# The last rows of wo in a decode kernel: the last row in two halves, row 0 added ahead of the merge

## The chip, the cores and the metric

One core of one Trainium2 chip runs the whole kernel. The metric is device microseconds of one execution, the median over several runs. The profiler also gives one execution in detail: which instruction ran when on which engine, what it waited for, and what the DMA engines moved.

## The reference

One decode step mixes two branches for two batch rows: attention over a cache of 4096 keys and values for 32 heads, and a small feed-forward branch with SiLU.

```
g = _sigmoid((x * gate_w).sum(-1, keepdims=True))
q = (x @ wq).reshape(B, Sq, H, Dh)          # B=2, Sq=1, D=640, H=32, Dh=128
p = softmax(einsum("bhqd,bhkd->bhqk", q, k_cache) * Dh ** -0.5)
a = einsum("bhqk,bhkd->bhqd", p, v_cache).reshape(B, Sq, H * Dh) @ wo    # wo: 4096 x 640
b = silu(x @ w1) @ w2
out = g * a + (1 - g) * b                    # 2 x 1 x 640
```

All data is float32. Keys and values are 268 MB together, wo is 10.5 MB.

## The kernel before

The heads go in groups of four (HQ = 8), with two batch rows: 16 items. For each item a key slab and a value slab of 128 partitions by 16384 numbers are loaded; GpSimd and VectorE multiply keys by the query, VectorE sums to scores, ScalarE exponentiates, TensorE multiplies weights by values. The results, scaled by the gate, stand in the tile oP, 32 columns for each row of wo that a partition holds.

After the last item comes the projection by wo. Every partition holds 32 rows of wo in four groups (NP = 4) of PR = 8 rows, each of 640 numbers. Groups 0 to 2 go to the slab v, the last group (g = 3) to the slab b. `load_wo` issues six DMAs from SyncE's queue: groups 0 and 1 together, group 2 in two pieces, group 3 in three (rows 0 to 4, rows 5 and 6, row 7). A float32 matmul shows in the trace as two matmul records, two passes one after the other.

- `in_halves` (L556) takes a row in two halves of 320 columns, in two strips of 32 PSUM partitions, and adds it up in the bank ps_acc (`early`), where the feed-forward branch already stands. Groups 0 and 1 use two pairs of strips at once; group 2 uses one pair.
- `merge` (L568, L573): ScalarE copies `early` to SBUF (`partial`), and four matmuls with the constant `join` sum the halves up into the bank ps_0 (`acc`), now in four strips of 160 columns.
- `in_quarters` (L586) takes each row of the last group in four strips of 160 columns, straight into `acc`.
- VectorE copies `acc` to SBUF (`ot`, L891), and SyncE's last DMA stores it to the output in pieces of 640 bytes.

The order on each engine is the order of the code. `Flow.op` finds the waits: an operation waits for the last writer of what it reads and for the readers of what it writes. Of PSUM banks it has a rule more, which the prediction needs:

```
if r.startswith("ps_"):
    deps += [d for d in self.readers.get(r, ()) if d.eng != eng]
```

So an engine that reads a PSUM bank waits for readers of the same bank on other engines that stand ahead of it in the code. A wait of TensorE for a piece of wo stands ahead of the first matmul that reads the piece, and holds up whatever TensorE has behind it.

Of the kernel before, what the change touches and what calls it, by code (L numbers as in the profile page):

```python
# [5 lines left out]
ALU = mybir.AluOpType  # L6
AX = mybir.AxisListType
# [151 lines left out]
def gated_decode(nc, x, kc, vc, wq, wo, w1, w2, gate, out):  # L159
    P = 128  # L160
    B, H, SK, DH = kc.shape
    D = x.shape[2]
# [13 lines left out]
    HB = 16  # L176
    CV = 68
    G = 4
    W = D // G
    W2 = D // 2  # L180
    NP = HQ // 2
    PR = 2 * Q
    FIRST = 5
    LEAD = HB // 2
    PACED = (NP - 2) * PR
    items = [(hq, b) for hq in range(HQ) for b in range(B)]
# [3 lines left out]
    s_out, s_sent = nc.alloc_semaphore("output"), nc.alloc_semaphore("sent")  # L190
    f = Flow(nc)
    V, S_, T_, G_ = nc.vector, nc.scalar, nc.tensor, nc.gpsimd

    def sb(name, shape, align=32):
        return nc.alloc_sbuf_tensor(name, shape, F32, align_bytes=align)[tuple([slice(None)] * len(shape))]

    def bank(name):
        return nc.alloc_psum_tensor(name, [P, 512], F32)[:, :]
# [4 lines left out]
    slab = {n: slabs[:, k * SLAB : (k + 1) * SLAB] for k, n in enumerate("vba")}  # L203

    def part(n, *ks):
        return [f"{n}.{k}" for k in (ks or range(8))]
# [13 lines left out]
    g = sb("g", [P, B])  # L220
# [4 lines left out]
    he = sb("he", [P, FR, B])  # L225
    seq = sb("seq", [P, 2 * FR, HB])
    join = sb("join", [P, 2, HB + 1])
    turned = sb("turned", [P, FR * 32])
    mask = sb("mask", [P, B])
    spaced = sb("spaced", [P, FR, 32])  # L230
# [7 lines left out]
    row = sb("row", [64, DH])  # L238
    oP_xs = sb("oP_xs", [P, LEAD + NP * PR * 32 + D // Q])
    oP, xs = oP_xs[:, : -D // Q], oP_xs[:, -D // Q :]  # L240
# [3 lines left out]

    ps_q, ps_o, ps_v, ps_acc, ps_t, ps_m, ps_0, ps_1 = (bank(f"ps{i}") for i in range(8))
    oT = ps_m[:64, 256:512].rearrange("p (n r) -> p n r", r=32)
    early, acc = ps_acc[:, :W2], ps_0[:, :W]

    h_q, h_e, h_v, h_o = (f.sem(n) for n in ("next_q", "weights", "values", "rows"))

# [4 lines left out]
    PD = PR * D  # L255


    partial = slab["v"][:, (NP - 1) * PD :][:, :W2]
    ot = slab["v"][:, (NP - 1) * PD + W2 :][:, :W]

    def kslab(i):
        return "a" if i % 2 == 0 else "b"
# [21 lines left out]
    def load_wo(g):  # L284

        n, at = ("v", g * PD) if g < NP - 1 else ("b", 0)
        if g == 0:
            src = wo[: 2 * PR * P, :].rearrange("(g p n) d -> p g (n d)", g=2, n=PR)
            to = slab["v"][:, : 2 * PD].rearrange("p (g c) -> p g c", g=2)
            f.dma("SP", to, src, writes=part("v", 0, 1), after=v_users)  # L290
            return
        if g == 1:
            return
        src = wo[g * PR * P : (g + 1) * PR * P, :].rearrange("(p n) d -> p (n d)", n=PR)
        cuts = (0, PD // 2, PD) if g < NP - 1 else (0, FIRST * D, PD - D, PD)
        after = f.users(part(n)) if g == NP - 1 else v_users
        for k, (c0, c1) in enumerate(zip(cuts, cuts[1:])):
            f.dma("SP", slab[n][:, at + c0 : at + c1], src[:, c0:c1], writes=part(n, g % (NP - 1) + k), after=after)
# [11 lines left out]
        writes=part("v", 0),  # L310
# [7 lines left out]
            out=ident, in_=ident, compare_op=ALU.not_equal, fill=1.0, base=0, pattern=[[-1, P]], channel_multiplier=1  # L318
        ),
        reads=["ident"],  # L320
        writes=["ident"],
# [2 lines left out]
    f.op("POOL", lambda: G_.memset(pz, 0.0), writes=["pz"])  # L324
    f.op("POOL", lambda: G_.memset(seq, 0.0), writes=["seq"])

    out_rows = out.rearrange("b s (n d) -> (s n) b d", n=G)
    f.dma("SP", out_rows, oP[0:P:HB, :W], reads=["oP"], writes=["out"])

    f.op("DVE", lambda: V.memset(ones, 1.0), writes=["ones"])  # L330
    f.op(
# [2 lines left out]
        reads=["ident"],  # L334
        writes=["block"],
# [6 lines left out]
        reads=["block"],  # L342
        writes=["fold"],
# [4 lines left out]
        reads=["ident"],  # L348
        writes=["sel"],
# [4 lines left out]
        reads=["ident"],  # L354
        writes=["half"],
# [7 lines left out]
            axis=AX.X,  # L363
        ),
        reads=["sel"],
        writes=["pick"],
# [4 lines left out]
        reads=["sel"],  # L371
        writes=["own"],
# [4 lines left out]
        reads=["ident"],  # L377
        writes=["side"],
# [6 lines left out]
        reads=["block"],  # L385
        writes=["spread"],
# [4 lines left out]
        reads=["ident"],  # L391
        writes=["mask"],
    )
    f.op("DVE", lambda: V.memset(join, 0.0), writes=["join"])
    for e in range(2):
        ends, at = join[:, e, ::HB], 64 + HB * (1 - e)
# [5 lines left out]
            reads=["ident", "join"],  # L402
            writes=["join"],
        )
        for t in (at, at + 32):
# [3 lines left out]
                reads=["ident", "join"],  # L409
                writes=["join"],  # L410
            )

    H_AT = FH * HD
    X_AT = H_AT + B * F
# [4 lines left out]
        reads=["xs0", "xs1"],  # L421
        writes=["xt"],
# [5 lines left out]
        reads=["xt"],  # L428
        writes=["gx"],
# [7 lines left out]
    for b in range(B):  # L437
        for j in range(J):
            at = xt[:, j, HB * b : HB * b + 1]
# [11 lines left out]
                reads=part("a") + ["xt"],  # L451
                writes=[f"hsum{b}"],
            )

    def mm_hr():
# [18 lines left out]
        reads=["ones", "gp"],  # L474
        writes=["ps_o"],
# [7 lines left out]
        reads=["g"],  # L483
        writes=["gc"],
# [7 lines left out]
    for e in range(2):  # L492
# [3 lines left out]
            reads=["ps_v"],  # L496
            writes=[f"spaced{e}"],
# [8 lines left out]
        reads=["he", "gc"],  # L506
        writes=["he"],
    )
    for e in range(2):
# [5 lines left out]
            reads=["he", "turned", "half", "seq"],  # L515
            writes=[f"seq{e}"],
# [27 lines left out]
    def heads(g):  # L544
        return [f"oP{g}{u}{b}" for u in range(2) for b in range(B)]

    def in_halves(g):

        for k in range(PR):
            s_ = g * PR + k  # L550

            def fn(k=k, s_=s_):
                to = 64 * (s_ % 2) if s_ < PACED else 0
                for n in range(2):
                    at = 32 * s_ + LEAD // 2 * n
                    last = T_.matmul(  # L556
                        early[to + 32 * n : to + 32 * n + 32, :],
                        oP[:, at : at + 32],
                        slab["v"][:, s_ * D + n * W2 : s_ * D + (n + 1) * W2],
                        start=(s_ == 0),  # L560
                        stop=(s_ in (PACED - 1, PACED + PR - 1)),
                    )
                return last

            f.op("PE", fn, reads=part("v", g + (g == NP - 2 and k >= PR // 2)) + heads(g), writes=["ps_acc"])

    def merge():
        f.op("ACT", lambda: S_.copy(partial, early), reads=["ps_acc"], writes=["partial"])  # L568

        def fn():  # L570
            for n in range(G):
                e, c = divmod(n * W, W2)
                last = T_.matmul(  # L573
                    acc[32 * n : 32 * n + HB + 1, :], join[:, e, :], partial[:, c : c + W], start=True, stop=False
                )
            return last

        f.op("PE", fn, reads=["partial", "join"], writes=["ps_0"])

    def in_quarters(g):  # L580
        for k in range(PR):
            at = LEAD + 32 * (g * PR + k)

            def fn(k=k, at=at):
                for n in range(G):
                    last = T_.matmul(  # L586
                        acc[32 * n : 32 * n + HB + 1, :],
                        oP[:, at : at + HB + 1],
                        slab["b"][:, k * D + n * W : k * D + (n + 1) * W],
                        start=False,  # L590
                        stop=(k == PR - 1),
                    )
                return last

            f.op("PE", fn, reads=part("b", (k >= FIRST) + (k == PR - 1)) + heads(g), writes=["ps_0"])

    ffn_out("v")

# [40 lines left out]
    def copy_q(i):  # L639
        f.op("ACT", lambda: S_.copy(qsb, ps_q[:, :DH]), reads=["ps_q"], writes=["qsb"])  # L640

    f.op("PE", mm_qr, reads=part("v", 1) + part("b") + ["xz"], writes=["ps_0", "ps_1"])
    for u in range(2):
        for b in range(B):
# [7 lines left out]
                reads=[f"ps_{u}", "mask"],  # L652
                writes=[f"qall{u}{b}"],
# [199 lines left out]
    for i in range(N + 1):  # L853
# [22 lines left out]
        if i == N - 1:  # L876
            v_users = f.users(part("v"))
            for g_ in range(NP):
                load_wo(g_)
# [4 lines left out]
        if i + 1 < N:  # L884
            query(i + 1, by=[ops["relay", i]], loop=i)
            copy_q(i + 1)
    for g_ in range(NP - 1):
        in_halves(g_)
    merge()
    in_quarters(NP - 1)  # L890
    f.op("DVE", lambda: V.tensor_copy(ot, acc), reads=["ps_0"], writes=["ot"])  # L891
    f.dma("SP", out_rows, ot[0:P:HB, :], reads=["ot"], writes=["out"], signal=s_out)


    def land():
# [15 lines left out]
    f.plan()  # L911
    for e in ("SP", "POOL"):
        f.run(e)
    spans = {"ACT": (14, 34), "DVE": (100, 220), "PE": (len(f.ops["PE"]) - NP * PR - 1, len(f.ops["PE"]))}
    for e, (a, b) in spans.items():
        ops, at = f.ops[e], 0
        while at < len(ops):
            end = at
            if at == a:
                f.once(e, ops[a:b])  # L920
                at = b
            elif ops[at].loop is None:
# [3 lines left out]
                at = end  # L926
            else:
# [3 lines left out]
                at = end  # L931
# [21 lines left out]
```

## Time and profile before

| | before |
|---|---|
| median of 3 runs | 695.7 us (695.59 to 695.74) |
| span of the profiled execution | 694.2 us |
| what lies around the span, against the median | 1.5 us |
| TensorE, VectorE, ScalarE, GpSimd busy | 30%, 73%, 6%, 38% of the span |
| moved from memory | 298.26 MB, 430 GB/s over the span |

The profiled execution has no time of its own on record beside its span, so a span is set against the median with the 1.5 us as a constant. Times within the execution are us from the start of the span. Busy shares are means over a long loop and a short end; what this change touches is the last six us.

### The profile page before, as it was taken

What the parts mean: (1) busy time and instruction counts of PE and PEld (TensorE: products, weight loads), DVE (VectorE), ACT (ScalarE), POOL (GpSimd) and SP (SyncE); (2) the same over time, 40 slices, a digit from 0 to 9 for tenths busy, and PEclk for the clock granted to TensorE, in tenths of its full rate; (3) what the DMA queues carried; (4) which work ended last, traced back from release to release, by engine and by line L of the source; (5) the groups of instructions that cost most, each with busy time, mean ns of one, the idle gap of its engine ahead of it and who ended that gap; (6) DMA issues with size and microseconds to landing.
All of it is one profiled execution on the core that took longest, in us unless ns stands there. A gap on an engine that the chain in (4) does not pass through costs nothing. (4 is left out here: it accounts for less than half of the span.)

```text
span 694.2 us, 3593 instructions
## 1 busy us (share of the span) xinstructions
PE 211.4 (30%) x1440; PEld 72.5 (10%) x1440; DVE 507.5 (73%) x269; ACT 40.0 (6%) x152; POOL 265.6 (38%) x26
## 2 busy tenths in 40 slices
PE   0074032151331405060412306060503315050657
PEld 0032010010110101020100101010100101010113
DVE  3810958898989596886959596986959595977811
ACT  0001010101010101010010101010000101010000
POOL 1000808191726090815335180906244270907100
PEclk9998556565565757575665757575655757575689
DMA  9999999999999999999999999999999999999997
GB/s 383 430 446 450 430 427 424 423 457 438 427 430 423 430 461 427 434 423 423 438 457 427 430 423 427 464 430 430 423 423 461 434 430 427 423 438 457 427 408 326
DMA packets 6209, 298.33 MB, mean 430 GB/s; under 512 B 672, under 2 KB 700, under 8 KB 956
## 3 DMA queue, kind: packets, MB, share of 16 engines
q1 hardware_dynamic: 6204, 298.27, 99.4%
q8 instruction: 2, 0.03, 0.0%
q14 instruction: 3, 0.02, 0.0%
HBM read 298.26 MB, written 0.01 MB: 430 GB/s over the span
## 5 line engine op out<-in xcount | busy, mean ns | idle before, releaser
L670 POOL TENSOR_TENSOR slabs<-slabs,qsb 128x7680 f32<-128x7680 f32 x16 | 262.3, 16396 | 378.7 <-DMA slabs<-in_A_k_cache_dram 347.8
L686 DVE TENSOR_REDUCE s<-slabs 128x68 f32<-128x8704 f32 (+1 forms) x32 | 276.3, 8676 | 0.0
L766 PE MATMUL ps<-slabs,pz 128*32 128x512 f32 x1024 | 146.2, 735 | 345.2 <-PEq L145 338.2
L676 DVE TENSOR_TENSOR slabs<-slabs,ps 128x8704 f32<-128x8704 f32 x16 | 147.5, 9218 | 108.5 <-DMA slabs<-in_A_k_cache_dram 108.4
L766 PEld LDWEIGHTS ps<-slabs,pz 128*32 128x32 f32 x1024 | 39.5, 132 | 438.6 <-issue 431.6
L715 ACT ACTIVATE pz<-s,nb 32x128 f32<-32x128 f32 x64 | 25.4, 398 | 556.5 <-PE ps L766 363.2
L804 PE MATMUL ps<-osb,pick 128*128 128x512 f32 x32 | 20.4, 724 | 58.9 <-PEq L145 58.0
L818 DVE TENSOR_REDUCE row<-ps 64x128 f32<-64x512 f32 x16 | 10.9, 682 | 23.3 <-PE ps L804 23.3
L788 DVE SCALAR_TENSOR_TENSOR osb<-ps,rg,own 128x512 f32<-128x512 f32 x16 | 12.0, 748 | 21.4 <-PE ps L766 21.2
L618 PE MATMUL ps<-qall,spread 128*128 (+1 forms) x32 | 7.4, 319 | 35.3 <-PEq L145 34.5
L446 DVE SCALAR_TENSOR_TENSOR slabs<-slabs 128x1728 f32<-128x1728 f32 x8 | 16.1, 2019 | 0.3
L458 PE MATMUL ps<-slabs,xz_col 128*32 128x432 f32 x16 | 3.1, 928 | 33.2 <-DVE slabs L446 33.2
L804 PEld LDWEIGHTS ps<-osb,pick 128*128 128x128 f32 x32 | 5.4, 211 | 73.0 <-issue 71.2
L715 ACT ACTIVATION_READ_ACCUMULATOR pz<-s,nb 32x1 f32 x64 | 11.8, 184 | 0.0
L618 PEld LDWEIGHTS ps<-qall,spread 128*128 128x128 f32 x32 | 6.9, 224 | 44.9 <-issue 43.2
L533 PE MATMUL ps<-slabs,seq 128*32 128x320 f32 x54 | 10.3, 545 | 3.7 <-DVE seq L512 3.7
L825 DVE STREAM_TRANSPOSE ps<-row 64x256 f32<-64x256 f32 x16 | 10.3, 642 | 0.6
L608 PE MATMUL ps<-slabs,xz_col 128*32 128x512 f32 x80 | 9.8, 593 | 0.0
L891 DVE COPY slabs<-ps 128x160 f32<-128x160 f32 x1 | 0.3, 325 | 12.2 <-PE ps L586 12.2
L556 PE MATMUL ps<-slabs,oP_xs 128*32 128x320 f32 x96 | 8.8, 433 | 1.4 <-DMA slabs<-in_A_wo_dram 1.4
L740 PE MATMUL ps<-rs,fold 128*128 128x1 f32 x32 | 6.1, 260 | 2.3 <-PEq L145 2.1
L740 PEld LDWEIGHTS ps<-rs,fold 128*128 128x128 f32 x32 | 5.7, 222 | 5.0 <-issue 3.5
(63 smaller groups left out, 71.9 us busy)
## 6 DMA issues: line engine op xcount, KB each, us to landing
slabs<-in_A_wq_dram SPq DMA_DIRECT2D x1, 10240.0 KB, 44.5
slabs<-in_B_w_dram SPq DMA_DIRECT2D x2, 4320.0 KB, 17.0
slabs<-in_A_wo_dram SPq DMA_DIRECT2D x1, 5120.0 KB, 21.5
slabs<-in_A_wo_dram SPq DMA_DIRECT2D x2, 1280.0 KB, 25.4
slabs<-in_A_wo_dram SPq DMA_DIRECT2D x1, 1600.0 KB, 30.1
slabs<-in_A_wo_dram SPq DMA_DIRECT2D x1, 640.0 KB, 31.1
slabs<-in_A_wo_dram SPq DMA_DIRECT2D x1, 320.0 KB, 31.4
slabs<-in_A_k_cache_dram SPq DMA_DIRECT2D x16, 47.8
```

Source lines behind the costliest of these rows:

```text
L446: lambda b=b, j=j, at=at: V.scalar_tensor_tensor(hsum[:, b, :], w1t[:, j, :], at, hsum[:, b, :], op0=ALU.mult, op1=ALU.add)
L533: last = T_.matmul(early[to : to + 32, :], seq[:, k : k + 2, :].rearrange("p k z -> p (k z)"), slab[n][:, k * HD : (k + 1) * HD], start=(k ...
L618: return T_.matmul(ps_q[:, :DH], spread, qall.rearrange("p h b d -> p (h b) d")[:, i, :], start=True, stop=True,)
L670: lambda: G_.tensor_mul(k[:, CV:, :], k[:, CV:, :], qsb[:, None, :].to_broadcast([P, C - CV, DH])),
L676: lambda: V.tensor_mul(k[:, :CV, :], k[:, :CV, :], ps_q[:, None, :DH].to_broadcast([P, CV, DH])),
L686: lambda c0=c0, c1=c1: V.reduce_sum(Ss[i % 2][:, c0:c1], k[:, c0:c1, :], axis=AX.X),
L715: last = S_.activation(pz[lo:hi, :, 4 * q : 4 * q + 4], s[lo:hi].rearrange("p (g c) -> p g c", c=4), AF.Exp, bias=nb[lo:hi], scale=SCALE, ...
L740: lambda *_: T_.matmul(ps_t[:, :1], fold.rearrange("p a q c -> p (a q c)"), rs, start=True, stop=True),
L766: last = T_.matmul(ps_v[32 * q : 32 * q + 32, :], pz[:, gr, :], v[:, gr, :], start=(gr < 4), stop=(gr >= NG - 4),)
L788: lambda: V.scalar_tensor_tensor(osb, ps_v.rearrange("p (c d) -> p c d", d=DH), rg, own[:, :, None].to_broadcast([P, 4, DH]), op0=ALU.mult ...
L804: lambda *_: T_.matmul(ps_o, pick, osb.rearrange("p c d -> p (c d)"), start=True, stop=True),
L818: lambda: V.reduce_sum(row, ps_o[:64].rearrange("p (c d) -> p d c", d=DH), axis=AX.X),
```

## The change

Five things change together.

1. The last group's pieces are cut at rows 4, 6 and 7.5 instead of 5 and 7: four DMAs of 4, 2, 1.5 and 0.5 rows.
2. Row 0 of the last group (HALVED = 1) is taken by `in_halves` like the groups before it, so it goes to `early`, ahead of the merge.
3. A strip of the result now holds 80 columns of the first half of the 640 and 80 of the second, so the merge needs both halves in one matmul: ScalarE multiplies `early` by a mask (`side_of`) into the first half of `partial`, VectorE by the other mask into the second half, and four matmuls with `both` follow.
4. Row 7's first half goes to `acc` as 80 columns a strip; its second half goes apart into the bank ps_1 (`rest`). VectorE copies `acc` to `ot`, then adds `rest` to 80 columns of it.
5. The output's DMA has pieces of 320 bytes, twice as many. Two small VectorE operations at the program's start make `both` and `side_of`.

```diff
-    FIRST = 5
+    HALVED = 1
+    CUTS = (0, 4, 6)
...
-    early, acc = ps_acc[:, :W2], ps_0[:, :W]
+    early, acc, rest = ps_acc[:, :W2], ps_0[:, :W], ps_1[:, : W // 2]
...
-        cuts = (0, PD // 2, PD) if g < NP - 1 else (0, FIRST * D, PD - D, PD)
+        cuts = (0, PD // 2, PD) if g < NP - 1 else (*(k * D for k in CUTS), PD - W2, PD)
...
-    out_rows = out.rearrange("b s (n d) -> (s n) b d", n=G)
+    out_rows = out.rearrange("b s (e n d) -> (s n) b e d", e=2, n=G)
...
+    f.op("DVE", lambda: V.tensor_add(both, join[:, 0, :], join[:, 1, :]), reads=["join"], writes=["both"])
+    f.op("DVE", lambda: V.reduce_sum(side_of, join, axis=AX.X), reads=["join"], writes=["side_of"])
...
-        for k in range(PR):
+        last_row = NP * PR - PR + HALVED - 1
+        for k in range(PR if g < NP - 1 else HALVED):
             s_ = g * PR + k
...
+            w = slab["v"][:, s_ * D : (s_ + 1) * D] if g < NP - 1 else slab["b"][:, k * D : (k + 1) * D]
...
-        f.op("ACT", lambda: S_.copy(partial, early), reads=["ps_acc"], writes=["partial"])
+        f.op("ACT", lambda: S_.mul(partial[:, 0, :], early, side_of[:, 0:1]), reads=["ps_acc", "side_of"], writes=["partial0"])
+        f.op(
+            "DVE",
+            lambda: V.tensor_scalar(partial[:, 1, :], early, side_of[:, 1:2], None, op0=ALU.mult),
+            reads=["ps_acc", "side_of"],
+            writes=["partial1"],
+        )
...
+                    acc[32 * n : 32 * n + HB + 1, :],
+                    both,
+                    partial[:, :, n * W4 : (n + 1) * W4],
+                    start=True,
+                    stop=False,
...
-        for k in range(PR):
-            at = LEAD + 32 * (g * PR + k)
+        for k in range(HALVED, PR + 1):
+            r, cols = min(k, PR - 1), slice(k == PR, 1 + (k != PR - 1))
+            at = LEAD + 32 * (g * PR + r)
+            w = slab["b"][:, r * D : (r + 1) * D].rearrange("p (e n c) -> p n e c", e=2, n=G)
...
+                        rest[strip, :] if k == PR else to[strip, cols, :],
...
-    for g_ in range(NP - 1):
+    for g_ in range(NP):
         in_halves(g_)
     merge()
     in_quarters(NP - 1)
     f.op("DVE", lambda: V.tensor_copy(ot, acc), reads=["ps_0"], writes=["ot"])
-    f.dma("SP", out_rows, ot[0:P:HB, :], reads=["ot"], writes=["out"], signal=s_out)
+    f.op("DVE", lambda: V.tensor_add(ot[:, W4:], ot[:, W4:], rest), reads=["ot", "ps_1"], writes=["ot"])
+    f.dma("SP", out_rows, two_ends(ot), reads=["ot"], writes=["out"], signal=s_out)
```

On TensorE the end of the program stood as follows before: the second piece of group 2 (load_436), the merge, and then the last group's three pieces (load_437 to load_439). One row is a run of like matmuls.

```order
L556 MATMUL ps<-slabs,oP_xs 32x320 [waits load_436]
L556 MATMUL ps<-slabs,oP_xs 32x320 x7
L573 MATMUL ps<-slabs,join 17x160 [waits done_ACT]
L573 MATMUL ps<-slabs,join 17x160 x3
L586 MATMUL ps<-slabs,oP_xs 17x160 [waits load_437,done_DVE]
L586 MATMUL ps<-slabs,oP_xs 17x160 x19
L586 MATMUL ps<-slabs,oP_xs 17x160 [waits load_438]
L586 MATMUL ps<-slabs,oP_xs 17x160 x7
L586 MATMUL ps<-slabs,oP_xs 17x160 [waits load_439]
L586 MATMUL ps<-slabs,oP_xs 17x160 x3
```

After the change, the same place reads as below; the last group's four pieces are now load_439 to load_442, and the line numbers are those of the changed kernel.

```order
L570 MATMUL ps<-slabs,oP_xs 32x320 [waits load_439,done_DVE]
L570 MATMUL ps<-slabs,oP_xs 32x320
L592 MATMUL ps<-slabs,both 17x160 [waits done_DVE]
L592 MATMUL ps<-slabs,both 17x160 x3
L613 MATMUL ps<-slabs,oP_xs 17x160 x12
L613 MATMUL ps<-slabs,oP_xs 17x160 [waits load_440]
L613 MATMUL ps<-slabs,oP_xs 17x160 x7
L613 MATMUL ps<-slabs,oP_xs 17x160 [waits load_441]
L613 MATMUL ps<-slabs,oP_xs 17x160 x3
L613 MATMUL ps<-slabs,oP_xs 17x80 x4
L613 MATMUL ps<-slabs,oP_xs 17x80 [waits load_442]
L613 MATMUL ps<-slabs,oP_xs 17x80 x3
```

The merge stood ahead of the wait for the last group's first piece and now stands behind it; it waits for VectorE where it waited for ScalarE.

VectorE's last three instructions after the change (there was only the copy of 128x160, which waited for TensorE):

```order
L865 SCALAR_TENSOR_TENSOR oP_xs<-ps,side,oE 64x8 [waits done_DVE]
L585 TENSOR_SCALAR slabs<-ps,side_of 128x320 [waits done_ACT]
L919 COPY slabs<-ps 128x160 [waits done_PE]
L920 TENSOR_TENSOR slabs<-slabs,ps 128x80 [waits done_PE,done_DVE]
```

The new multiplication L585 waits for ScalarE, whose multiplication L582 reads the same PSUM bank and stands ahead of it; the addition L920 waits for the copy L919 as well as for TensorE.

## Rows read from the trace of the kernel before

**Rows 1.** The page: its first line, and the DMA share in 40 equal slices.

```profile
span 694.2 us, 3593 instructions
...
DMA  9999999999999999999999999999999999999997
```

**Rows 2.** The chain that ended last: start us, us, what.

```profile
658.74 0.43 SPq L69
...
659.21 30.07 DMA slabs<-in_A_wo_dram
689.28 0.14 issue
```

**Rows 3.** Timeline of the end: start, us, engine, line, operation, tiles, shapes, idle before.

```profile
687.76 0.44 PE L556 MATMUL ps<-slabs,oP_xs 128*32 128x320 f32 x2
688.25 0.43 ACT L568 COPY slabs<-ps 128x320 f32<-128x320 f32 x1 [28.38 <-PE ps L556]
...
688.73 0.47 PE L573 MATMUL ps<-slabs,join 128*17 128x160 f32 x8 [0.53 <-ACT slabs L568]
...
689.42 2.66 PE L586 MATMUL ps<-slabs,oP_xs 128*17 128x160 f32 x64 [0.23 <-DMA slabs<-in_A_wo_dram]
690.87 0.41 PEld L586 LDWEIGHTS ps<-slabs,oP_xs 128*17 128x17 f32 x16 [0.23 <-DMA slabs<-in_A_wo_dram]
691.61 0.13 PEld L586 LDWEIGHTS ps<-slabs,oP_xs 128*17 128x17 f32 x8 [0.34 <-DMA slabs<-in_A_wo_dram]
692.15 0.33 DVE L891 COPY slabs<-ps 128x160 f32<-128x160 f32 x1 [12.24 <-PE ps L586]
692.50 0.58 SPq L69 DMA_DIRECT2D out_dram<-slabs  x1
```

**Rows 4.** Stretches: us, each engine's busy time (instructions), granted clock, DMA share, GB/s.

```profile
660.30:667.20 6.90, 0.01 (x1) 0.00 (x0) 1.60 (x6) 0.00 (x0) 0.00 (x0) 0.74 0.90 390
667.20:670.50 3.30, 3.23 (x16) 0.80 (x20) 0.00 (x0) 0.00 (x0) 0.00 (x0) 0.50 1.07 459
...
677.99:679.39 1.40, 0.01 (x1) 0.00 (x0) 1.32 (x2) 0.00 (x0) 0.00 (x0) 1.00 0.98 417
679.39:688.20 8.81, 8.81 (x96) 3.84 (x96) 0.45 (x3) 0.00 (x0) 0.00 (x0) 1.00 1.01 428
689.40:690.80 1.40, 1.38 (x40) 1.21 (x40) 0.00 (x0) 0.00 (x0) 0.00 (x0) 1.00 0.70 280
```

**Rows 5.** Groups by line and shape: busy us, mean ns of one, idle before.

```profile
L788 DVE SCALAR_TENSOR_TENSOR osb<-ps,rg,own 128x512 f32<-128x512 f32 x16 | 12.0, 748 | 21.4 <-PE ps L766 21.2
...
L640 ACT COPY qsb<-ps 128x128 f32<-128x128 f32 x16 | 4.3, 267 | 5.9 <-PE ps L618 5.8
...
L586 PE MATMUL ps<-slabs,oP_xs 128*17 128x160 f32 x64 | 2.7, 301 | 0.2 <-DMA slabs<-in_A_wo_dram 0.2
L647 ACT ACTIVATE qall<-ps,mask 128x512 f32<-128x512 f32 x4 | 2.4, 689 | 20.3 <-PE ps L608 20.3
...
L586 PEld LDWEIGHTS ps<-slabs,oP_xs 128*17 128x17 f32 x64 | 1.7, 97 | 1.2 <-DMA slabs<-in_A_wo_dram 0.6 <-issue 0.5
...
L495 DVE COPY spaced<-ps 128x224 f32<-128x224 f32 x2 | 0.7, 382 | 0.0
...
L568 ACT COPY slabs<-ps 128x320 f32<-128x320 f32 x1 | 0.4, 426 | 28.4 <-PE ps L556 28.4
...
L505 DVE TENSOR_TENSOR he<-he,gc 128x28 f32<-128x28 f32 x1 | 0.2, 189 | 0.0
```

**Rows 6.** DMA issues from 659 to 690: KB, median us to landing (group 2's second piece).

```profile
slabs<-in_A_wo_dram SPq DMA_DIRECT2D x1, 1280.0 KB, 26.7
```

**Rows 7.** Timeline of VectorE near the program's start.

```profile
5.07 0.36 DVE L408 TENSOR_TENSOR join<-join,ident 128x2 f32<-128x2 f32 x2
5.47 0.17 DVE L399 TENSOR_REDUCE join<-ident 128x2 f32<-128x8 f32 x1
...
13.75 0.46 DVE L420 STREAM_TRANSPOSE slabs<-oP_xs 128x160 f32<-128x160 f32 x1 [7.72 <-DMA oP_xs<-in_gate_w_dram]
```

More of the change, by code (lines that the diff above doesn't have):

```diff
@@ L180, in gated_decode @@
     W2 = D // 2
+    W4 = W // 2
     NP = HQ // 2
     PR = 2 * Q
-    FIRST = 5
+    HALVED = 1
+    CUTS = (0, 4, 6)
     LEAD = HB // 2
@@ L227, in gated_decode @@
     join = sb("join", [P, 2, HB + 1])
+    both = sb("both", [P, HB + 1])
+    side_of = sb("side_of", [P, 2])
     turned = sb("turned", [P, FR * 32])
@@ L255, in gated_decode @@
     PD = PR * D
-    partial = slab["v"][:, (NP - 1) * PD :][:, :W2]
-    ot = slab["v"][:, (NP - 1) * PD + W2 :][:, :W]
+    partial = slab["v"][:, (NP - 1) * PD :][:, :D].rearrange("p (e c) -> p e c", e=2)
+    ot = slab["v"][:, (NP - 1) * PD + D :][:, :W]
     def kslab(i):
@@ L325, in gated_decode, with two_ends @@
     f.op("POOL", lambda: G_.memset(seq, 0.0), writes=["seq"])
-    out_rows = out.rearrange("b s (n d) -> (s n) b d", n=G)
-    f.dma("SP", out_rows, oP[0:P:HB, :W], reads=["oP"], writes=["out"])
+    out_rows = out.rearrange("b s (e n d) -> (s n) b e d", e=2, n=G)
+    def two_ends(t):
+        return t[0:P:HB, :W].rearrange("p (e d) -> p e d", e=2)
+    f.dma("SP", out_rows, two_ends(oP), reads=["oP"], writes=["out"])
     f.op("DVE", lambda: V.memset(ones, 1.0), writes=["ones"])
@@ L547, in in_halves, with fn @@
     def in_halves(g):
-        for k in range(PR):
+        last_row = NP * PR - PR + HALVED - 1
+        for k in range(PR if g < NP - 1 else HALVED):
             s_ = g * PR + k
-            def fn(k=k, s_=s_):
+            w = slab["v"][:, s_ * D : (s_ + 1) * D] if g < NP - 1 else slab["b"][:, k * D : (k + 1) * D]
+            which = part("v", g + (g == NP - 2 and k >= PR // 2)) if g < NP - 1 else part("b", 0)
+            def fn(s_=s_, w=w):
                 to = 64 * (s_ % 2) if s_ < PACED else 0
@@ L558, in fn @@
                         oP[:, at : at + 32],
-                        slab["v"][:, s_ * D + n * W2 : s_ * D + (n + 1) * W2],
+                        w[:, n * W2 : (n + 1) * W2],
                         start=(s_ == 0),
-                        stop=(s_ in (PACED - 1, PACED + PR - 1)),
+                        stop=(s_ in (PACED - 1, last_row)),
                     )
                 return last
-            f.op("PE", fn, reads=part("v", g + (g == NP - 2 and k >= PR // 2)) + heads(g), writes=["ps_acc"])
+            f.op("PE", fn, reads=which + heads(g), writes=["ps_acc"])
@@ L567, in merge @@
     def merge():
-        f.op("ACT", lambda: S_.copy(partial, early), reads=["ps_acc"], writes=["partial"])
+        f.op("ACT", lambda: S_.mul(partial[:, 0, :], early, side_of[:, 0:1]), reads=["ps_acc", "side_of"], writes=["partial0"])
[5 more added lines that the diff above has]
+        )
         def fn():
             for n in range(G):
-                e, c = divmod(n * W, W2)
@@ L573, in fn @@
                 last = T_.matmul(
-                    acc[32 * n : 32 * n + HB + 1, :], join[:, e, :], partial[:, c : c + W], start=True, stop=False
+                    acc[32 * n : 32 * n + HB + 1, :],
[3 more added lines that the diff above has]
+                    stop=False,
                 )
             return last
-        f.op("PE", fn, reads=["partial", "join"], writes=["ps_0"])
+        f.op("PE", fn, reads=["partial0", "partial1", "both"], writes=["ps_0"])
@@ L580, in in_quarters, with fn @@
     def in_quarters(g):
-        for k in range(PR):
-            at = LEAD + 32 * (g * PR + k)
-            def fn(k=k, at=at):
+        to = acc.rearrange("p (e c) -> p e c", e=2)
+        for k in range(HALVED, PR + 1):
+            r, cols = min(k, PR - 1), slice(k == PR, 1 + (k != PR - 1))
+            at = LEAD + 32 * (g * PR + r)
+            w = slab["b"][:, r * D : (r + 1) * D].rearrange("p (e n c) -> p n e c", e=2, n=G)
+            def fn(k=k, at=at, w=w, cols=cols):
                 for n in range(G):
+                    strip = slice(32 * n, 32 * n + HB + 1)
@@ L586, in fn @@
                     last = T_.matmul(
-                        acc[32 * n : 32 * n + HB + 1, :],
+                        rest[strip, :] if k == PR else to[strip, cols, :],
                         oP[:, at : at + HB + 1],
-                        slab["b"][:, k * D + n * W : k * D + (n + 1) * W],
-                        start=False,
-                        stop=(k == PR - 1),
-                    )
-                return last
-            f.op("PE", fn, reads=part("b", (k >= FIRST) + (k == PR - 1)) + heads(g), writes=["ps_0"])
+                        w[:, n, cols, :],
@@ L597, in gated_decode @@
+                        start=(k == PR),
+                        stop=(k >= PR - 1),
+                    )
+                return last
+            piece = sum(k >= c for c in CUTS[1:]) + (k == PR)
+            f.op("PE", fn, reads=part("b", piece) + heads(g), writes=["ps_1" if k == PR else "ps_0"])
     ffn_out("v")
@@ L913, in gated_decode @@
         f.run(e)
-    spans = {"ACT": (14, 34), "DVE": (100, 220), "PE": (len(f.ops["PE"]) - NP * PR - 1, len(f.ops["PE"]))}
+    spans = {"ACT": (14, 34), "DVE": (102, 222), "PE": (len(f.ops["PE"]) - NP * PR - 2, len(f.ops["PE"]))}
     for e, (a, b) in spans.items():
```

## The prediction

> **What bounds the kernel now.** I read the page first. The DMA engines are full in every slice but the last [rows 1]: 298 MB have to come in, and nothing in the long loop is touched by this change. So the question is only what stands between the last bytes and the end. For that I read the chain that ended last, then the timeline of the last six us, and the reader should see who waits for whom there.
>
> The chain runs through one DMA: the last group's first piece is issued at 659.21 and lands 30.07 later, at 689.28 [rows 2]. TensorE starts on its five rows at 689.42, waits again before 690.87 (rows 5 and 6) and before 691.61 (row 7), each time for a piece of wo [rows 3]. So TensorE is faster than the landings and is idle ahead of each; the end is set by the landing of row 7 plus a short tail. That tail is: matmuls to 692.08 (689.42 + 2.66), VectorE's copy 692.15 to 692.48, the store's issue at 692.50, and 1.70 from there to the end of the span at 694.2 [rows 1, 3].
>
> The work ahead is hidden before: TensorE ends group 2 at 688.20, ScalarE copies `early` from 688.25 for 0.43, and the merge runs from 688.73 for 0.47, to 689.20 [rows 3]. That is 0.08 before the first piece lands. The cover is thin, and the merge does not depend on the last group at all.
>
> **What the change does to it.** On TensorE, row 0 of the last group now stands ahead of the merge, and it needs a piece that lands late. So ScalarE's and VectorE's multiplications, the merge, and seven rows behind it in TensorE's queue all wait for that landing. I follow this chain step by step.
>
> *The first piece.* It has four rows instead of five. Group 2's second piece is issued at 658.74 and takes 26.7 to land, at 685.44 [rows 2, 6]; the five rows behind it take 689.28 - 685.44 = 3.84, or 0.77 a row. Four rows land at 688.51. I allow 0.1 either way, as the pieces come on many DMA engines that end apart.
>
> *Row 0.* TensorE started 0.14 after the landing at 689.28 [rows 2, 3], with the same two semaphores to wait for: 688.65. In the stretch to 688.20, 16 rows that go two at a time and 8 single ones make 32 steps of a pass over 320 columns, in 8.81 of which the last step's matmuls take 0.44: (8.81 - 0.44) / 31 = 0.27 a step [rows 3, 4]. Two passes end 0.27 + 0.44 later, at 689.36. If the start costs only 0.04, it is 0.10 less.
>
> *ScalarE's multiplication* starts 0.05 after, as the copy did [rows 3]: 689.41. The copy of 320 columns took 426 ns, that of 128 columns 267: 0.83 ns a column [rows 5]. The multiplication by a column of numbers is nearest to the 689 ns at 512 columns, so 689 - 192 x 0.83 = 530 ns; bounds 0.43 (as the copy) and 0.69. It ends at 689.94.
>
> *VectorE's multiplication* waits for ScalarE, since both read ps_acc. I take 0.05 for the handover, which is what ScalarE to TensorE took (688.25 + 0.43 to 688.73 [rows 3]). VectorE's copies out of PSUM took 325 ns for 160 columns and 382 for 224, 0.89 ns a column [rows 3, 5], so 320 columns take 0.47; bounds 0.38 and 0.75, the copy of 224 and the row with 512 columns [rows 5]. It ends at 690.46. In the trace of before no two engines read one bank so close together. The Trainium skill, "PSUM — Partial Sum Buffer", section "PSUM bank collisions raise a hardware error", says that two engines must not access one bank at the same time, two reads included; no run here shows it. By that rule the wait has to be there and the sum stays; without the wait the two would overlap and the sum would be 0.5 less, 696.2.
>
> *Merge and rows 1 to 6.* TensorE starts 0.05 later, at 690.51. Five rows took 1.38 [rows 4], 0.276 a row; the merge's matmuls have the same shape. Seven such units take 1.93, to 692.44. The pieces no longer matter: rows 4 and 5 land by about 690.05 (halfway from 689.28 to 690.83, where 690.83 is 690.87 less the same 0.04 that I allow for a start), row 6 and half of row 7 at about 691.2, the rest by about 691.6. TensorE comes to them at 691.61, 692.16 and later, so it never waits. This is the turn: TensorE, not the DMA, sets the end. The fourth piece costs one more issue, 0.43 on SyncE's queue at about 661 [rows 2], some 28 us ahead of its landing: nothing. GpSimd's queue has no change.
>
> *Row 7.* Its two parts have 80 columns, half of 160, so 0.14 each if the columns set it and 0.276 if nothing does. A weight load takes 97 ns [rows 5] and two follow one another on each strip, 0.19, so I take 0.20. The first part's last matmul starts 0.10 + 0.02 into it. A record took 301 ns at 160 columns and 0.44 at 320 [rows 3, 5], 0.87 ns a column; 80 columns take 0.23 to 0.24. The first part ends at 692.80, the second, 0.20 later, at 693.00.
>
> *VectorE's end.* The copy of 160 columns starts 0.07 after, as it did (692.08 to 692.15 [rows 3]), and takes 0.33: 692.87 to 693.20. So the second part of row 7 is hidden behind this copy. The addition waits for the copy: the handover from one VectorE instruction to the next is 0.04 (5.07 + 0.36 to 5.47 [rows 7]). Its time does not stand in the trace; 28 columns took 189 ns [rows 5], with 0.89 ns for each of 52 more that is 0.24; bounds 0.19 and 0.38. It ends at 693.48, and the store is issued at 693.50, against 692.50.
>
> *The store* has sixteen pieces of 320 bytes instead of eight of 640. No row shows it; I take the 1.70 as it is.
>
> *The start.* The two added VectorE operations have the shapes of rows that took 0.17 to 0.18 each [rows 7], and lie in the 7.72 that VectorE then waits for a DMA: nothing.
>
> **The sum.** 693.50 - 692.50 = +1.0. The span goes from 694.2 to 695.2, and with the 1.5 us around it the time from 695.7 to **696.7 us**. The bounds of all terms at once are +0.5 and +1.7; they will not all fall on one side, so the likeliest case's own range is 696.4 to 697.2.
>
> What the change gives is in this sum, but small: after the last landing half the columns are left for TensorE, and VectorE adds 80 columns where it copied 160, 0.24 for 0.33. But the copy of 160 is now an instruction ahead of the addition, so even with TensorE free the tail hardly shrinks (the first rival).
>
> **The rivals.** 0.2% of 695.7 is 1.4 us, which is about what a measurement of this kernel can tell from no change; 697.1 and 694.3 are the borders.
>
> *The merge stays hidden, and the last landing sets the end.* TensorE must then be free when row 6 and half of row 7 land at 691.2. Row 6 takes 0.28 and the first part of row 7 ends 0.36 behind that: 691.88 with the start. Copy 691.95 to 692.28, addition 692.32 to 692.56, store at 692.58, +0.08: 695.8 us. For this the merge would have to start by 691.2 - 6 x 0.276 = 689.5, and I have it at 690.51. Row 0 and the two multiplications would have to take a third of what their rows say. Against it speaks nearly every row; for it only that no row shows the multiplications. Chance 0.10.
>
> *The store gets slower: the case that ends beyond the border.* From its issue to the end it takes 1.70, of which 0.58 is the issue [rows 3] and 1.12 transfer and closing. Should the smaller pieces double the latter, 1.12 comes on top of the 1.0: 697.8 us. It passes the border when the store loses 0.4. No row has pieces of 320 bytes, so only the smallness of the store (5 KB) speaks against it. Beside this: the Trainium skill, "DMA: Bandwidth & Descriptors", section "Specifications", states that below 512 bytes the engine reads, modifies and writes; no transfer of before shows it. Chance 0.08.
>
> *TensorE's clock falls.* Its new idle stretches are 688.20 to 688.65 and 689.36 to 690.51. After 6.90 us with TensorE idle the granted clock was 0.50, the lower of the two levels, 1.2 GHz; after 1.40 us of idleness at 677.99 it stayed 1.00, 2.4 GHz [rows 4]. The new gaps are shorter than that. At the lower level the seven units and row 7's first half, 1.93 + 0.10, would take twice as long: +3.0 in all, 698.7 us. Chance 0.05.
>
> **How the numbers follow.** The forecast has 0.77, of which 0.06 lies above 697.1. Slower by over 0.2%: 0.06 + 0.08 + 0.05 = 0.19. Within: 0.71 of the forecast, and 0.08 of the first rival's 0.10. Its other 0.02 is left for faster by over 0.2%, which no mechanism here reaches. For the range I take 695.9 to 697.4: nearly all of the forecast, and some of both sides.
>
> **What would show it.** In the profile after: row 0's matmuls start near 688.65, VectorE's multiplication follows ScalarE's and does not overlap it, the merge starts near 690.5, and no idle time of TensorE for a DMA stands behind it. The chain that ended last names TensorE and ScalarE where it named a DMA only, and the last addition starts right behind the copy. The forecast is wrong if TensorE still waits for the last piece, if the time from the store's issue to the end is not 1.7, or if the granted clock falls behind 689.

## The result and the profile after

The changed kernel takes 697.0 us (median of 15 runs, 696.69 to 697.96), the kernel before beside it 695.74 (15 runs). The ratio is 1.0018, 95% interval 1.001 to 1.0025: slower by 1.26 us, 0.18%, inside the 0.2% that the prediction took as the border, and close to it. The forecast was 696.7, its range 695.9 to 697.4. A second set on another chip gave 696.84 against 695.73, ratio 1.0017 (1.0008 to 1.0026):

> The changed kernel once more, on the chip of the two others: for the scatter of the landings and for the ratio on one chip. 697.0 us; landings within 0.2 of the first profile, the merge near 690.8.

Every run also has its span. Their median is 695.5 after, in both sets; before it is 694.4 to 694.6 in the four sets of runs beside the experiments. The spans scatter less than the times, so below I give both. What lies around the span is 1.3 to 1.4 us in the median, before and after.

The page of the changed kernel begins so (line 1 and, from part 3, the loads of instructions on queue 8), to be held against [rows 1]; the page of the kernel before has the same line of queue 8:

```profile
span 695.5 us, 3607 instructions
...
q8 instruction: 2, 0.03, 0.0%
```

The chain that ended last in the changed kernel (start us, us, what) answers to [rows 2]:

```profile
657.75 0.43 SPq L69
...
658.23 30.52 DMA slabs<-in_A_wo_dram
688.74 0.14 issue
688.88 0.75 PE ps L570 x4
...
689.65 0.54 ACT slabs L582
...
690.21 0.56 DVE slabs L585
...
690.82 0.47 PE ps L592 x8
691.28 1.81 PE ps L613 x56
...
693.12 0.34 DVE slabs L919
693.46 0.02 issue
693.48 0.24 DVE slabs L920
```

The reader sees the DMA end at 688.74 with the four rows of the last group's first piece, and behind it one unbroken row of engines: row 0 on TensorE, ScalarE's multiplication, VectorE's, the merge, the rows left, copy, addition. Before, the DMA stood in the chain to 689.28 and TensorE waited for pieces after that.

The timeline (start, us, engine, line, operation, idle before and its releaser) shows that no wait for a DMA is left behind row 0's; [rows 3] had two more, before 690.87 and 691.61:

```profile
688.88 0.73 PE L570 MATMUL ps<-slabs,oP_xs 128*32 128x320 f32 x4 [0.46 <-DMA slabs<-in_A_wo_dram]
...
691.10 2.09 PE L613 MATMUL ps<-slabs,oP_xs 128*17 128x160 f32 x64
693.12 0.33 DVE L919 COPY slabs<-ps 128x160 f32<-128x160 f32 x1 [2.36 <-PE ps L613]
693.48 0.24 DVE L920 TENSOR_TENSOR slabs<-slabs,ps 128x80 f32<-128x80 f32 x1
693.74 0.58 SPq L69 DMA_DIRECT2D out_dram<-slabs  x1
```

The stretches (us, busy time of TensorE, weight load, VectorE, ScalarE, GpSimd with counts, granted clock, DMA share, GB/s) answer to [rows 4]:

```profile
688.40:688.88 0.48, 0.02 (x3) 0.03 (x1) 0.00 (x0) 0.00 (x0) 0.00 (x0) 1.00 1.10 453
689.61:690.82 1.21, 0.01 (x2) 0.01 (x1) 0.55 (x1) 0.53 (x1) 0.00 (x0) 1.00 0.57 214
691.10:692.73 1.63, 1.63 (x57) 1.41 (x48) 0.00 (x0) 0.00 (x0) 0.00 (x0) 1.00 0.03 11
692.73:693.18 0.45, 0.45 (x24) 0.26 (x12) 0.06 (x1) 0.00 (x0) 0.00 (x0) 1.00 0.08 18
```

In 689.61 to 690.82 TensorE does nothing, ScalarE is busy 0.53 and VectorE 0.55, one after the other, while the DMA engines bring in nearly all that is left. When TensorE comes back, at 690.82, it has 1.63 us of rows and row 7 before it; the DMA share in that stretch is 0.03. The granted clock stays 1.00 in all four stretches, so the rival of the falling clock did not happen.

### The profile page after: what moved, and what is told of

It is laid out like the page before. It is cut to its first block, busy times and chain, and to the rows that moved or that the text cites. A ratio compares the mean times of both kernels' runs of the same rounds, so it can differ in the third digit from the quotient of the medians.

```text
span 695.5 us, 3607 instructions
## 1 busy us (share of the span) xinstructions
PE 209.7 (30%) x1444; PEld 72.6 (10%) x1444; DVE 508.7 (73%) x273; ACT 40.1 (6%) x152; POOL 266.2 (38%) x26
## 5 line engine op out<-in xcount | busy, mean ns | idle before, releaser
L585 DVE TENSOR_SCALAR slabs<-ps,side_of 128x320 f32<-128x320 f32 x1 | 0.6, 550 | 9.6 <-ACT slabs L582 9.6
## 6 DMA issues: line engine op xcount, KB each, us to landing
slabs<-in_A_wo_dram SPq DMA_DIRECT2D x3, 1280.0 KB, 27.9
```

## The experiments

Two theories stood against the reading that the merge waits for a landing (theory 1 below): that the added work costs its time wherever it stands (theory 2), and that four pieces land later than three (theory 3). The pieces of one execution land earlier or later than those of another: the first piece of four rows lands between 688.56 and 688.74 in the two profiles of the changed kernel, with four rows ahead and without the addition, and at 689.61 in the kernel with one copy (last section). So where the chain starts at the landing of the last group's first piece, I compare the time from that landing to the store's issue: 3.22 before (689.28 to 692.50), 5.00 after (688.74 to 693.74). These two differ by 1.78 and not by the 1.24 between the stores, since a first piece of four rows lands earlier than one of five; kernels with equal pieces compare directly. The landing is read from the chain of each kernel, as in the first lines above; it lies 0.14 ahead of the first matmul that reads the piece.

| kernel | time, the kernel before beside it | ratio, 95% interval | median span, before's | around the span |
|---|---|---|---|---|
| row 0 back | 696.52, 695.93 | 1.0009 (1.0 to 1.0018) | 694.7, 694.5 | 1.7 |
| hidden merge | 696.59, 696.04 | 1.0006 (0.9997 to 1.0015) | 694.8, 694.6 | 1.6 |
| one copy, row 0 ahead | 696.56, 695.93 | 1.0009 (1.0 to 1.0018) | 695.2, 694.5 | 1.4 |
| no addition | 696.76, 696.04 | 1.001 (1.0001 to 1.0019) | 695.3, 694.6 | 1.5 |
| hidden merge, no addition | 695.91, 696.04 | 1.0 (0.9991 to 1.0009) | 694.6, 694.6 | 1.4 |
| four rows ahead | 697.57, 695.93 | 1.0027 (1.0016 to 1.0037) | 696.25, 694.5 | 1.3 |
| before, row 0 ahead | 697.12, 695.93 | 1.0019 (1.001 to 1.0028) | 695.6, 694.5 | 1.4 |
| merge in the slack | 699.27, 695.73 | 1.0047 (1.0033 to 1.0061) | 694.3, 694.4 | 5.0 |
| before, idle matmuls | 695.99, 695.73 | 1.0003 (0.9994 to 1.0012) | 694.6, 694.4 | 1.4 |
| ScalarE takes both | 698.96, 695.81 | 1.0039 (1.0027 to 1.0051) | 694.4, 694.45 | 4.7 |
| two idle matmuls | 697.52, 695.81 | 1.0026 (1.0016 to 1.0037) | 694.45, 694.45 | 3.0 |

**The kernel before, with row 0 alone put ahead of the merge.** Pieces, strips, the one copy and the store are those of before.

```diff
-        for k in range(PR):
+        for k in range(PR if g < NP - 1 else HALVED):
...
-        for k in range(PR):
+        for k in range(HALVED, PR):
...
-    for g_ in range(NP - 1):
+    for g_ in range(NP):
         in_halves(g_)
```

> The kernel before with one part of the change alone: row 0 of the last group goes ahead of the merge; three pieces, ScalarE's one copy, strips and store as before. Theory 1: the first piece has five rows and lands at 689.28, row 0 ends at 690.15, the merge starts near 690.67 and eight units of 0.27 follow; the store is issued near 693.45, and the time is 696.6 us (+0.9). Theory 2: no work is added, 695.8 us.

Timeline of this kernel, row 0 to the store:

```profile
689.53 0.73 PE L560 MATMUL ps<-slabs,oP_xs 128*32 128x320 f32 x4 [1.22 <-DMA slabs<-in_A_wo_dram]
690.30 0.42 ACT L572 COPY slabs<-ps 128x320 f32<-128x320 f32 x1 [31.61 <-PE ps L560]
690.77 0.47 PE L577 MATMUL ps<-slabs,join 128*17 128x160 f32 x8 [0.52 <-ACT slabs L572]
...
693.56 0.58 SPq L69 DMA_DIRECT2D out_dram<-slabs  x1
```

The first piece landed 0.14 ahead of 689.53, at 689.39, and the store follows 4.17 behind it, as expected (689.28 to 693.45) and 0.95 more than before's 3.22. The median span is 1.1 longer, the time 1.2 where 0.9 was expected. So this one move, without any of the other changes, costs about what the whole change costs. The two other theories gave it nothing. Row 0, copy and merge now put 1.71 (689.53 to 691.24) ahead of the other rows, where one row took 0.28; TensorE's former waits of 0.23 and 0.34 for pieces [rows 3] take up 0.57 of that. The move also makes the row longer, as the experiment with four rows shows.

**The changed kernel with row 0 back.**

```diff
-    HALVED = 1
+    HALVED = 0
```

> The changed kernel with HALVED = 0: row 0 of the last group goes back behind the merge, all else stays as changed (four pieces, two multiplications, the addition, the small store). Theory 1, the merge waits for the last group's first piece: the two multiplications run from 688.25 to about 689.4, the merge from 689.4, seven rows behind it; the store is issued at about 692.6, and the time is 695.9 us (+0.1 to +0.2). Theory 2, the added work costs its time wherever it stands: most of the 1.3 us stays, about 696.7 us. Theory 3, four pieces land later than three: the pieces land 0.2 later than before here too, and at least 0.2 of the loss stays.

Its timeline:

```profile
688.41 0.53 ACT L582 ACTIVATE slabs<-ps,side_of 128x320 f32<-128x320 f32 x1 [28.69 <-PE ps L570]
688.97 0.55 DVE L585 TENSOR_SCALAR slabs<-ps,side_of 128x320 f32<-128x320 f32 x1 [7.49 <-ACT slabs L582]
689.57 0.47 PE L592 MATMUL ps<-slabs,both 128*17 128x160 f32 x8 [1.21 <-DVE slabs L585]
689.86 2.36 PE L613 MATMUL ps<-slabs,oP_xs 128*17 128x160 f32 x72
...
692.77 0.59 SPq L69 DMA_DIRECT2D out_dram<-slabs  x1
```

The merge starts at 689.57 instead of 690.82, since ScalarE starts right behind group 2. The span falls by 0.8, to 0.2 above before, as the first theory had it. The two multiplications still end behind the first piece's landing, at 688.68 in this trace, so TensorE has no idle time from the merge on and this kernel is still bound by it, but only just. The time fell less than the span: 0.6 above before, of which 0.4 lies around the span (below). So the expected time of 695.9 was missed, and by the time alone, 696.5, this run does not tell theory 1 from theory 2, which had 696.7; the span and the trace do.

**Four rows ahead of the merge.**

```diff
-    HALVED = 1
+    HALVED = 4
```

> The changed kernel with HALVED = 4: rows 0 to 3 of the last group go ahead of the merge, all in the same first piece. Theory 1: three more rows of 0.54 ahead of the merge, three of 0.27 less behind it, 0.8 in all; the merge starts 1.6 later behind the landing, and the time is 697.8 us. Theory 2 and 3, which do not speak of the merge's place: 697.0 us.

```profile
688.79 2.35 PE L570 MATMUL ps<-slabs,oP_xs 128*32 128x320 f32 x16 [0.45 <-DMA slabs<-in_A_wo_dram]
...
692.34 0.47 PE L592 MATMUL ps<-slabs,both 128*17 128x160 f32 x8 [1.20 <-DVE slabs L585]
...
694.45 0.58 SPq L69 DMA_DIRECT2D out_dram<-slabs  x1
```

The piece landed at 688.65, the store follows 5.80 behind it, 0.80 more than the 5.00 of the changed kernel; expected were 0.8. The median span is 0.75 above that of the changed kernel. The expected 697.8 us was not quite reached: measured were 697.6. Three rows cost 0.27 each, since a row takes 0.54 in halves and 0.276 in quarters. This shows that TensorE sets the end here; it does not tell the theories apart, as work that costs its time wherever it stands would give the same 0.8.

**One copy instead of two multiplications, row 0 still ahead.** ScalarE copies `early` once, the merge takes `join` in eight matmuls of 80 columns, and a product of zeros starts `acc` while TensorE is idle ahead of the projection.

```diff
-        f.op("ACT", lambda: S_.mul(partial[:, 0, :], early, side_of[:, 0:1]), ...)
-        f.op("DVE", lambda: V.tensor_scalar(partial[:, 1, :], early, side_of[:, 1:2], ...), ...)
+        f.op("ACT", lambda: S_.copy(partial[:, 0, :], early), reads=["ps_acc"], writes=["partial0"])
...
+                        acc[32 * n : 32 * n + HB + 1, e * W4 : (e + 1) * W4],
+                        join[:, e, :],
+                        partial[:, 0, n * W4 : (n + 1) * W4],
```

> The changed kernel with row 0 still ahead of the merge, but ScalarE copies early once, without VectorE, and the merge takes join in eight matmuls of 80 columns; TensorE starts acc with a product of zeros ahead of the projection, where it is idle. Theory 1: the chain loses VectorE's multiplication of 0.55 with its handover and ScalarE's 0.53 becomes 0.43, so the merge starts about 0.69 earlier behind the landing, the store is issued near 693.05, and the time is 696.3 us. If the two multiplications cost nothing, it stays at 697.0.

```profile
689.74 0.73 PE L570 MATMUL ps<-slabs,oP_xs 128*32 128x320 f32 x4 [0.80 <-DMA slabs<-in_A_wo_dram]
690.51 0.43 ACT L582 COPY slabs<-ps 128x320 f32<-128x320 f32 x1 [30.36 <-PE ps L570]
690.99 0.50 PE L587 MATMUL ps<-slabs,join 128*17 128x80 f32 x16 [0.52 <-ACT slabs L582]
...
693.92 0.59 SPq L69 DMA_DIRECT2D out_dram<-slabs  x1
```

From the landing at 689.61 to the store it is 4.31, against 5.00: 0.69 less, as expected. The absolute store time was missed (693.92 for 693.05), as the pieces landed later here; the time, 696.6 for 696.3, carries that with it. What goes with it is below.

**No addition.** Row 7's second half is added up in `acc` too, and one copy ends it.

```diff
-                        rest[strip, :] if k == PR else to[strip, cols, :],
+                        to[strip, cols, :],
...
-    f.op("DVE", lambda: V.tensor_add(ot[:, W4:], ot[:, W4:], rest), reads=["ot", "ps_1"], writes=["ot"])
```

> The changed kernel with row 7's second half added up in acc by TensorE too, and one copy of 160 columns at the end: the addition of 0.24 is gone, the copy waits 0.14 longer. TensorE's end is unchanged, so the store comes about 0.13 earlier: 696.9 us. If the addition is hidden, nothing changes: 697.0.

```profile
693.24 0.33 DVE L919 COPY slabs<-ps 128x160 f32<-128x160 f32 x1 [2.50 <-PE ps L613]
693.59 0.58 SPq L69 DMA_DIRECT2D out_dram<-slabs  x1
```

The first piece landed at 688.72, so the store comes 4.87 behind it: 0.13 less than after, as expected. The median span is 0.2 below the changed kernel's, the time 696.8 for 696.9. Summing the second half apart is therefore a loss of 0.13 in this place, since the copy of 160 columns stays on the path and the addition of 0.24 comes behind it, while TensorE needs only 0.14 more.

**The merge hidden**, with the one copy of the experiment before last and row 0 behind the merge, the addition kept; and the same **without the addition**, by the edit just shown.

```diff
-    HALVED = 1
+    HALVED = 0
```

> Row 0 behind the merge (HALVED = 0) and ScalarE's one copy with join in eight matmuls of 80 columns; four pieces, the addition and the small store as changed. The merge is hidden ahead of the first piece, as before. Then the last landings set the end: the copy of acc waits for the first part of row 7, the addition for the copy; the store is issued 0.9 to 1.0 behind the last landing, as before (0.93), and the time is 695.8 us. If the added columns on VectorE were what the change wins, it would be 695.5.

> The version that the readings point to: row 0 behind the merge, ScalarE's one copy, the merge hidden, row 7's last half in acc, one copy at the end. After the last landing only 80 columns in two passes and the copy are left: the store comes 0.78 behind the last landing against 0.93 before, and the time is 695.6 us, if the fourth piece does not land later; with landings 0.2 later it is 695.8.

The chain of the first names the DMA to 691.96 and VectorE behind TensorE's first part of row 7:

```profile
659.67 32.29 DMA slabs<-in_A_wo_dram
...
692.00 0.65 PE ps L608 x16
...
692.68 0.34 DVE slabs L921
...
693.03 0.24 DVE slabs L922
```

From that landing (row 6 and half of row 7) to the store at 693.30 it is 1.34; the first rival of the prediction put 1.38 there (691.2 to 692.58) and said that this is no gain over before. The expected time, 695.8, was missed: measured were 696.6, with the median span 0.2 above before's and 1.6 around it. The landing is late here, at 691.96, where the same piece lands at 691.53 in the next kernel and at 691.39 in the one after it. Without the addition the chain is

```profile
660.46 31.07 DMA slabs<-in_A_wo_dram
...
691.58 0.79 PE ps L608 x24
...
692.39 0.33 DVE slabs L921
```

with the store at 692.74, 1.21 behind the landing at 691.53: again 0.13 less. Its span and time equal before's (ratio 1.0, 0.9991 to 1.0009; 695.9 for the expected 695.6 to 695.8). So four pieces, the other strips and the small store cost nothing that can be told where the merge is hidden. And even with the merge hidden and the addition gone, half a row less behind the last landing is worth nothing that can be told.

**The merge in the slack.** No product of zeros: row 0 starts `acc`, the merge stands behind rows 0 to 3 on TensorE, both multiplications stay, no addition.

```diff
+    in_quarters(NP - 1, range(4))
     merge()
-    in_quarters(NP - 1)
+    in_quarters(NP - 1, range(4, PR + 1))
```

> The changed kernel with no row ahead of the merge, the merge put behind rows 0 to 3 of the last group on TensorE (row 0 starts acc), and row 7's last half in acc with one copy at the end; both multiplications stay. They run while rows 0 to 3 do, so the merge finds its input ready and TensorE waits for the last two pieces again. The store comes 0.82 behind the last landing, against 0.93 before; the fourth piece costs 0.04, so the time is 695.7 us, the same as before within what can be told. If the two multiplications or the merge were a cost wherever they stand, it is 696.5 or more.

```profile
689.01 0.55 DVE L585 TENSOR_SCALAR slabs<-ps,side_of 128x320 f32<-128x320 f32 x1 [7.52 <-ACT slabs L582]
689.95 0.47 PE L592 MATMUL ps<-slabs,both 128*17 128x160 f32 x8
...
691.44 0.74 PE L613 MATMUL ps<-slabs,oP_xs 128*17 128x160 f32 x24 [0.38 <-DMA slabs<-in_A_wo_dram]
692.25 0.32 DVE L920 COPY slabs<-ps 128x160 f32<-128x160 f32 x1 [2.69 <-PE ps L613]
692.60 0.59 SPq L69 DMA_DIRECT2D out_dram<-slabs  x1
```

Within the span all went as said: VectorE's 0.55 ran under rows 0 to 3, the merge waited for nothing, TensorE waits for the DMA again at the end, and the median span is 694.3, 0.1 below before. So the two multiplications, the merge and the fourth piece cost nothing where they are hidden; the theory of the added work falls for the span. The fourth piece makes the last landing 0.03 to 0.04 later: it comes 6.15 behind that of group 2's second piece in the two kernels with three pieces and 6.18 to 6.19 with four, where no load of instructions comes near 684 (last section). But the time is 3.5 us longer, all of it around the span, which no theory had. Three more kernels bear on that.

> The kernel before with twelve matmuls more (24 in the trace) on TensorE ahead of the projection, where it is idle; they add up nothing that is used. If a longer program for TensorE brings one more load of instructions through a DMA engine near 684, as in the three kernels with a product of zeros, the page shows three such loads on queue 8 instead of two, group 2 and what follows land up to 0.9 later, and the time is about 696.3 us. If it was something else in those three, 695.8 us.

> e8_merge_in_slack, whose span was no longer than before's but whose time was 3.5 us longer because of what lies around the span, with both multiplications on ScalarE: VectorE's program is one instruction shorter, ScalarE's one longer, nothing on the path changes. The span stays at 694.3. If the load of instructions that the trace shows behind the end of e8 is what lies around it, and hangs on the length of one engine's program, the rest around the span is back at 1.3 and the time is 695.6 us; if it hangs on something else of e8 (the order of the merge, the copy), it stays near 699.3.

> e8_merge_in_slack with two matmuls more (four in the trace) on TensorE ahead of the projection, where it is idle; they add up nothing that is used. The span stays at 694.3, or has one more load of instructions in it and is up to 0.9 longer. If the load behind the end hangs on the length of TensorE's program, the rest around the span changes from 5.0; if on VectorE's alone, it stays at 5.0 and the time near 699.3 us.

The edits: in the kernel before, `for n in 3 * list(range(G))` around a product of zeros ahead of the projection; in the merge in the slack, `S_.mul(partial[:, 1, :], early, side_of[:, 1:2])` on ScalarE for VectorE's `tensor_scalar`; there again, a product of zeros with two matmuls. What they showed stands in the last section.

## Why the prediction was right

The step on which it stood, that the last group's first piece now gates the merge and all behind it, was shown from both sides: row 0's move alone costs 0.95 from landing to store in the kernel before, and taking it back gives 0.8 us of span in the changed one. The two multiplications and the fourth piece cost the span nothing when the merge is hidden again. The turn from DMA to TensorE as what sets the end is in the chain after.

The terms, against the trace. The first piece landed at 688.74 for 688.51. Of the 0.23, 0.21 was there before: group 2's second piece, issued at 657.75, took 27.9 to land by this row of the DMA issues, so it landed at 685.65 where it was 685.44.

```profile
slabs<-in_A_wo_dram SPq DMA_DIRECT2D x3, 1280.0 KB, 27.9
```

The step of 0.77 a row held. The lateness is scatter: in the second profile of the changed kernel the first piece landed at 688.56, and the span is 695.3. Row 0 took 0.73 for 0.71, ScalarE's multiplication 0.53 as forecast, the addition 0.24 as forecast, the seven units from 690.82 to 692.73 took 1.91 for 1.93. Two sizes were off. **VectorE's multiplication** took 0.55 where I took 0.47, carried over from copies by the column; it lies inside the bounds of 0.38 and 0.75. **Row 7's parts** took half of a row's 0.276, as columns alone would have it, where I had taken 0.20 for the weight loads: the fourth stretch above has 0.45 for both parts with the last drain. The first size made the sum too small, the second too large. The store came at 693.74 for 693.50, of which the late landing is 0.23. The later pieces landed late as well, row 6 and half of row 7 at 691.41 for 691.2, the rest at 691.82 for 691.6; TensorE came to them later still, so this cost nothing.

The store, with its 16 pieces of 320 bytes, took 1.7 from issue to the end as before, so that rival fell. The Trainium skill, "DMA: Bandwidth & Descriptors", section "Specifications", states that below 512 bytes the engine reads, modifies and writes. No cost of that shows at 320 bytes: 693.74 to 695.5 against 692.50 to 694.2. That VectorE waits for ScalarE on ps_acc is in the timeline, 0.03 behind the other's end; whether the two could read at once was not tried. The first rival, a hidden merge, was made by hand, and its arithmetic held from the landing on. One reading of it was wrong: for a hidden merge, row 0 and the two multiplications would have had to shrink from 1.71 by 1.01, so to two fifths of what their rows say and not to a third.

The forecast time, 696.7, was 0.3 under the measured one. The spans differ by 1.1 in the median, near the sum of 1.0; the medians of the times by 1.26. The forecast span of 695.2 is 0.3 under the median of 695.5, partly because the one profile of before, with 694.2, lies 0.2 to 0.4 under the median spans there; the forecast time does not hang on that, as it adds 1.0 to the median of the times.

## What to carry to other kernels

Before moving a piece of work ahead of a step on an in-order engine, ask what it waits for: one row moved past the merge made a hidden chain of copy and merge wait for a late landing, and that cost more than the row. To shorten the tail behind the last landing can pay only if everything ahead of it ends before that landing; here the cover was 0.08 us, and even with the merge hidden half a row less gave nothing that the time shows. And an instruction that takes 80 columns of a copy's 160 off the end gains nothing while the copy itself stands in front of it.

## What was not expected

In the kernel before the trace has no load of instructions on queue 8 near the end or behind it. In the merge in the slack there is one of 0.02 MB behind the end; this is the stretch from 695 to 700, with a span of 694.3:

```profile
q8 instruction: 1, 0.02, 1.7%
```

ScalarE's version has the same, and in both some 4.7 to 5.0 us lie around the span in the median instead of 1.3. Both have 1448 matmul records on TensorE; before it is 1440, after 1444. With four records more (two idle matmuls, 1452) the load moves in front of the end, into the stretch from 693 to 696, and 3.0 lie around the span. With 1460 to 1464 (one copy with row 0 ahead, the two hidden merges, before with idle matmuls) it comes between 682 and 686, and the rest is back at 1.4 to 1.6. There it goes with another price, late pieces of wo. The first piece of four rows lands at 689.61 with one copy, at 689.29 in the hidden merge and at 688.87 there without the addition, for 688.56 to 688.74 in the kernels without this load. The chain and the page of the kernel before with its idle matmuls:

```profile
q8 instruction: 3, 0.05, 0.0%
```

```profile
658.19 31.53 DMA slabs<-in_A_wo_dram
...
692.03 0.51 PE ps L586 x8
```

The wait for row 7 ends at 692.03 instead of 691.61, and the median span is 0.2 longer; the time, 1.0003 (0.9994 to 1.0012), can't tell it. That the load takes its time from wo is the likely reason for the late pieces, but it was not tried apart from the longer program. So a longer program on TensorE mostly goes with an earlier load, and a load at the very end goes with up to 3.6 us that no span shows. The number of records alone does not settle it: row 0 back has 1448 too, its trace has no load near the end or behind it, and only 1.7 lie around the span. Nor was it shown that the load itself holds up the end. The profile of the hidden merge has a second load at 696.8, 1.8 behind the end of its span, and that execution has 2.6 around it. The cause stays open. It follows that a gain of a tenth of a us in a span says little here until the time says it too, and no version here is clearly faster than the kernel before in time.
